# Decay attention, then a feed-forward block: the decay of all jobs from POOL, and the weights converted by block from the second job on

## The chip, the cores and the metric

The kernel runs on one core of one Trainium2 chip. The metric is device time in microseconds (us), the median of the runs. A core has five engines that run side by side, each working through its own list of instructions in order: PE (TensorE, matmuls), DVE (VectorE), ACT (ScalarE), POOL (GpSimd) and SP (which here issues DMAs). POOL and ACT issue DMAs too. All DMAs of the core share 16 DMA engines.

## The reference

Causal attention with a forget gate on 8 batches of 8 heads (576 positions, head size 64), then a feed-forward block on the 4608 resulting rows of 512:

```python
scores = (q @ k.T) / sqrt(64)
cum = cumsum(log(clip(f, 1e-4, 1)))
scores = where(causal, -1e9, scores + cum[i] - cum[j])
attn = exp(scores - max); attn = attn / (sum + 1e-9)
x = attn @ v                                   # (4608, 512)
h = x @ w_in                                   # w_in 512 x 2048
g = h if h >= 1, 0 if h <= -1, else (h + 1)**2 / 4
out = g @ w_out                                # w_out 2048 x 512
```

`w_in` and `w_out` come as 64-bit floats (8 MB each); everything else is 32-bit.

## The kernel before, in words

**Jobs.** The attention is cut into jobs of one pair of heads each (`jobs`; job `p`). Batch 0 has eight jobs: 0 to 3 take rows 0 to 255 of its four head pairs, 4 to 7 take rows 256 to 575. From job 8 on a job is a whole head pair, four jobs to a batch, 36 in all. A job works in blocks of 128 rows (`r`; the last has 64). For a row block, `scores` (L486) makes the products on PE in PSUM, `weights` (L589) takes the row minimum on DVE (L604), the exponential on ACT (L608), normalises, and splits the result into two f16 parts `pr` (ACT L622, DVE L628, or POOL L626); a transposing DMA on SP (L634, L637) brings them to `pT`, and `values` (L641) multiplies with v. Jobs 0 to 4 do the turning on PE instead (`turn_rows`, `early_values`). The values leave PSUM through ACT and DVE (L583/L584 or L657/L658) into `x`.

**The decay.** `decay_sums` (L149) makes the cumulative sums `cum` of log f for all heads and writes them to dram as `cum_d`. There are two ways in which the decay enters the scores. For jobs 0 to 7 (`NDEC`) the sums of batch 0 are also split into three bf16 parts, written to dram as `dec_d`, and each job loads its six rows through SP (`load_decay`, L407; the DMA is L416) into a buffer of the tag `vm`; two more bf16 matmuls per row block add the decay on PE (L511), and the causal mask comes from the prepared tiles `hide` in the minimum on DVE. From job 8 on `load_decay` fetches one row of `cum_d` per head, spread over all partitions, into `ck` (three buffers, POOL's queue, L411); in `scores` POOL makes scale times `ck` plus the row's own sum (L521) and masks the diagonal block (L525), and DVE takes the minimum over that plus the PSUM.

**Scales.** The f16 parts need powers of two as scales. `value_scale(b)` (L274) and `query_scale(b)` (L299) read all of v, q or k of a batch once more in four loads of 288 KB each (POOL's queue; L282, L306) into `vm` buffers, of which there are two, reduce each on DVE (L283, L307), and take the maximum over partitions with `across` (L117: a transpose and a small matmul on PE with small DVE instructions between).

**Weights.** The feed-forward width is cut into 8 blocks of 256. A block of each matrix is 1 MB of 64-bit floats; `weight_load` (L213) fetches it raw on SP into slots (`RAW`), which are partly places where other blocks will lie later; `weight_split` (L225) turns it into 32-bit with three DVE bit operations per quarter (L232, L235, L238), finds a bound (largest magnitude on DVE, L248, for `w_in`; sum of magnitudes on ACT, L252, for `w_out`), takes it through `across`, makes a scale, and writes a high f16 part (ACT L259) and the rest (POOL L261 and L262 for `w_in`, DVE L264 for `w_out`). One call handles one matrix of one block: 16 calls. `CONVERT` says in which job how many are made (jobs 3 to 7), `LOADS` and `AHEAD` how far ahead raw data is fetched.

**Feed-forward.** A unit is 256 rows (`ch`) by one block (`fb`): `moe_front` (L675: 24 or more matmuls into `ph`, then Relu, Square, a DVE clamp L701, and the two f16 parts of g, L703, L704) and `moe_back` (L711: 12 matmuls into `po`). There are 144 units. After each row block of a job so many units are run that those whose rows are ready get used up over four jobs; chunk 0 runs in three groups of blocks (`EARLY`), so that it can begin before all weights are there.

**Order.** The program is written in this order, job by job, with the loads of job p+2 and the preparation of job p+1 in job p. The compiler's scheduler then fixes each engine's list ahead of time: an instruction may be placed long before its turn in the program, once its inputs and a buffer are to be had by the scheduler's own reckoning, and buffers of one tag are handed out in the program's order. At run time each list is worked through in order.

Of the kernel before, what the change touches and what calls it, by code (L numbers as in the profile page):

```python
# [9 lines left out]
F16 = mybir.dt.float16  # L10
BF16 = mybir.dt.bfloat16
I32 = mybir.dt.int32
# [4 lines left out]
P = 128  # L17
# [14 lines left out]
NQK = 12  # L32
NDEC = 8

# [15 lines left out]
def kernel(  # L50
# [9 lines left out]
):  # L60

# [80 lines left out]
    nc.gpsimd.memset(ones, 1.0)  # L142
    NR = 6
    NDH = NDEC // (2 * NPAIR) * H
    dec_d = dram.tile([NDH, NR, 2, S], BF16, name="dec_d")
    cum_d = dram.tile([B * H, S], F32, name="cum_d")
    cq8 = const.tile([P, NT5, B * H], F32, name="cq8")

    def decay_sums():  # L149

        fl = early
        nb = B * H
        nc.sync.dma_start(fl[0:nb, 0:S], f.rearrange("b h s -> (b h) s"))
        rows = one.tile([P, NT5, 2, 2, S], F16, name="pT").rearrange("p t l h s -> p (t l h s)").bitcast(BF16)
        rows = rows[0:NDH, 0:NR * 2 * S].rearrange("p (r j s) -> p r j s", r=NR, j=2)
        nc.gpsimd.memset(fl[0:nb, 3 * S:4 * S], 0.0)
        nc.gpsimd.memset(rows[:, 1::2, 0], 1.0)
        nc.gpsimd.memset(rows[:, 0::2, 1], 1.0)
# [3 lines left out]
        nc.scalar.activation(fl[0:nb, S:2 * S], fl[0:nb, 0:S], AF.Ln)  # L162
        cum = fl[0:nb, 2 * S:3 * S]
# [11 lines left out]
        nc.sync.dma_start(dec_d, rows)  # L175
        nc.sync.dma_start(cum_d, cum)
        pt = ps1.tile([P, 1024], F32, name="big")
        twice = fl[0:nb, S:S + P]
# [12 lines left out]
    hides = one.tile([P, 2, 2, SP], F16, name="qs").rearrange("p j l e -> p (j l e)").bitcast(F32)  # L191
    hide, hide4 = hides[:, 0:FULL], hides[:, FULL:FULL + S]
    for t, h in ((hide, 1), (hide4, 2)):
        n = P // h
        wide = t.shape[1]
        nc.gpsimd.memset(t, 0.0)
        for i in range(h):
            a = t[n * i:n * i + n, wide - n:wide]
            nc.gpsimd.affine_select(
                a, a, pattern=[[-1, n]], channel_multiplier=1, base=0, compare_op=ALU.is_ge, fill=MASKED  # L200
            )

# [7 lines left out]

    def weight_load(n):  # L213
        i, j = divmod(n, 2)
        if j == 0:
            src = w_in.bitcast(I32)[:, i * 4 * P:(i + 1) * 4 * P].rearrange("(t p) c -> p t c", p=P)
        else:
            src = w_out.bitcast(I32)[i * 2 * P:(i + 1) * 2 * P, :].rearrange("(t p) c -> p t c", p=P)
        n = src.shape[1] // 2
        for k_, slot in enumerate(RAW[2 * i + j]):  # L220
            nc.sync.dma_start(
                slots[slot].rearrange("p (t c) -> p t c", t=n), src[:, n * k_:n * (k_ + 1), :]
            )

    def weight_split(n):  # L225
        i, j = divmod(n, 2)
        parts = []
        for k_, slot in enumerate(RAW[n]):
            top = slots[slot][:, 1::2]
# [10 lines left out]
            )  # L240
            parts.append((top.bitcast(F32), slice(k_ * DM, (k_ + 1) * DM)))
        hi = place[n][:, 0]
        lo = place[n][:, 1]
        m1 = tiny.tile([P, 1], F32, name="m1", bufs=2)
        ms = tiny.tile([P, 2], F32, name="ms", bufs=2)
        for k_, (wf, c) in enumerate(parts):
            if j == 0:
                nc.vector.tensor_reduce(  # L248
                    out=ms[:, k_:k_ + 1], in_=wf, axis=AX.X, op=ALU.max, apply_absolute_value=True
                )  # L250
            else:
                nc.scalar.activation(lo[:, c], wf, AF.Abs, accum_out=ms[:, k_:k_ + 1])  # L252
        nc.vector.tensor_reduce(out=m1, in_=ms, axis=AX.X, op=ALU.max)
        m = mi[:, i:i + 1] if j == 0 else tiny.tile([P, 1], F32, name="m2")
        across(m, m1)
        s = sw[:, j, i:i + 1]
        scale_of(s, mp[:, j, i:i + 1], m)
        for wf, c in parts:
            nc.scalar.activation(hi[:, c], wf, AF.Copy, scale=s)  # L259
            if n % 2 == 0:  # L260
                nc.gpsimd.tensor_scalar(out=wf, in0=wf, scalar1=s, scalar2=0.0, op0=ALU.mult, op1=ALU.add)  # L261
                nc.gpsimd.tensor_tensor(out=lo[:, c], in0=wf, in1=hi[:, c], op=ALU.subtract)  # L262
            else:
                nc.vector.scalar_tensor_tensor(  # L264
                    out=lo[:, c], in0=wf, scalar=s, in1=hi[:, c], op0=ALU.mult, op1=ALU.subtract
                )

# [139 lines left out]
    def load_decay(w, h):  # L407
        bh = w.b * H + 2 * w.hp + h
        if w.p >= NDEC:
            ck = two.tile([P, S], F32, name="ck", bufs=3)  # L410
            nc.gpsimd.dma_start(ck, cum_d[bh:bh + 1].broadcast_to([P, S]))  # L411
# [4 lines left out]
        nc.sync.dma_start(w.dec[64 * h:64 * h + NR], dec_d[bh])  # L416

# [68 lines left out]
    def scores(w, r):  # L486
# [15 lines left out]
        w.sds[r] = sds  # L502
        terms = [(x[:, s0:s1], y, D) for x, y in w.qk]
        if w.p < NDEC:
            terms.append((w.dec[:, 0, s0 + w.s0:s1 + w.s0], w.dec[:, 1], NR))
        for c0 in range(0, wid, 512):
            c1 = min(wid, c0 + 512)
            for i, (x, y, n) in enumerate(terms):
                for h in range(2):
                    rows = slice(64 * h, 64 * h + n)  # L510
                    nc.tensor.matmul(  # L511
                        outs[h][:, c0:c1], lhsT=x[rows], rhs=y[rows, c0:c1],
                        start=(i == 0), stop=(i == len(terms) - 1),
                    )
        if w.p < NDEC:
            return
        q0 = P * r
# [71 lines left out]
    def weights(w, r):  # L589
# [172 lines left out]
    def load_weights(n):  # L762
        nonlocal nload
        while nload < min(n, 2 * NB) and not any(set(RAW[nload]) & set(r) for r in RAW[nw:nload]):
            weight_load(nload)
            nload += 1

    def weight_step():
# [5 lines left out]
        for first, end in groups:  # L774
            if nw == 2 * end:
                z = moe_scales(0, first, end - 1, True)
# [13 lines left out]
    for p in range(njobs + 1):  # L790
# [42 lines left out]
        for i, st in enumerate(steps):  # L833
# [3 lines left out]
            while ready() and done - before < quota * (i + 1) // len(steps):  # L837
                if units[done] not in bsc and nw < 2 * NB:
                    break
                moe_unit(*units[done])  # L840
                done += 1
# [35 lines left out]
```

## Time and profile before

| | |
|---|---|
| median of 3 runs | 1243.08 us (1237.45 to 1243.55) |
| the profiled execution | 1248.13 us, span 1246.4 us, mean granted PE clock 0.93 |
| busy share of the span | PE 86%, DVE 67%, ACT 61%, POOL 35% |
| DMA | 163.27 MB, mean 131 GB/s |

The page of the profile gives busy times for each engine and, in 40 slices of 31 us, the busy share in tenths, the granted PE clock and the share of the DMA engines. Other views group instructions by line ("busy, mean ns of one, idle time before them and what ended it"), list them in order of time with their start and length, or give each engine's busy time between two points. In a name like `sdr<-ck,cq` the tile written stands first and those read behind it; PEld is PE's weight load; a suffix q (SPq, POOLq) marks an engine's issuing of DMAs.

### The profile page before, as it was taken

To read this page: it belongs to the slowest core of one execution; us is meant where nothing else is said; L and a number is where in the kernel's file an instruction comes from. 1 tells how busy PE (TensorE), PEld (TensorE's weight loads), DVE (VectorE), ACT (ScalarE), POOL (GpSimd) and SP (SyncE) were. 2 spreads that over 40 slices of the span, in tenths; PEclk is the share of its full clock that TensorE was granted. 3 is DMA by queue.
4 is the path that set the end of the run, shared out by engine and by line. 5 is a ranking of instruction groups with operands and counts; after the bars stand their busy time and mean duration, and the time that the engine had idled before them with its cause. 6 is when DMAs were issued, how large, how long until landed. Compare 5 with 4: busy or idle time off the path is not lost. (4 is left out here: it accounts for less than half of the span.)

```text
span 1246.4 us, 24524 instructions
## 1 busy us (share of the span) xinstructions
PE 1071.5 (86%) x8859; PEld 675.2 (54%) x8859; DVE 830.1 (67%) x2227; ACT 765.8 (61%) x1564; POOL 438.7 (35%) x752
## 2 busy tenths in 40 slices
PE   1569646798327988999999999999999999999998
PEld 1336333454215654665666666656566566667665
DVE  5747879788658777877765576687766877622222
ACT  2456545466436586777766676686777777734443
POOL 2021244464455463544532323454534444100000
PEclk9868767699667998999999999999999999999999
DMA  8822564598999888886756656577777675500000
GB/s 235 277 51 63 143 151 147 143 205 205 180 206 210 179 171 155 163 162 137 147 104 110 127 111 114 120 141 151 141 135 141 128 130 90 93 17 3 18 18 17
DMA packets 404906, 163.27 MB, mean 131 GB/s; under 512 B 384840, under 2 KB 384840, under 8 KB 404776
## 3 DMA queue, kind: packets, MB, share of 16 engines
q1 hardware_dynamic: 389040, 113.33, 48.6%
q0 software_dynamic: 10560, 38.94, 11.6%
q10 hardware_dynamic: 5184, 9.44, 2.1%
q8 instruction: 69, 1.13, 0.4%
q14 instruction: 53, 0.43, 0.1%
HBM read 86.61 MB, written 9.70 MB: 77 GB/s over the span
## 5 line engine op out<-in xcount | busy, mean ns | idle before, releaser
L690 PE MATMUL ph<-x,place 128*128 128x256 f16 (+3 forms) x4608 | 436.1, 249 | 36.9 <-DVE u L701 23.9
L718 PE MATMUL po<-place,g 128*128 128x512 f16 x1728 | 415.9, 383 | 7.1 <-ACT g L703 4.8
L690 PEld LDWEIGHTS <-place 128*128 128x128 f16 x4608 | 355.2, 99 | 115.7 <-issue 41.1
L718 PEld LDWEIGHTS <-g 128*128 128x128 f16 x1728 | 162.3, 99 | 181.3 <-issue 9.5
L521 POOL TENSOR_SCALAR sdr<-ck,nsig,cqs 128x128 f32<-128x128 f32 (+1 forms) x192 | 156.7, 820 | 290.4 <-DVE pr L628 278.0
L608 ACT ACTIVATE sdr<-sdr,nm 128x384 f32<-128x384 f32 (+1 forms) x248 | 137.8, 557 | 117.4 <-DVE nm L604 116.7
L701 DVE SCALAR_TENSOR_TENSOR u<-ph,z,u 128x512 f32<-128x512 f32 x136 | 101.5, 747 | 106.2 <-ACT u L700 105.8
L699 ACT ACTIVATE u<-ph,z 128x512 f32<-128x512 f32 x136 | 104.5, 768 | 76.3 <-PE ph L690 75.4
L628 DVE SCALAR_TENSOR_TENSOR pr<-sdr,rc,pr 128x384 f16<-128x384 f32 (+2 forms) x232 | 122.0, 561 | 38.9 <-ACT pr L622 36.2
L703 ACT ACTIVATE g<-u,z 128x512 f16<-128x512 f32 x136 | 97.7, 719 | 74.0 <-DVE u L701 73.5
L622 ACT ACTIVATE pr<-sdr,rc 128x384 f16<-128x384 f32 (+1 forms) x236 | 119.8, 556 | 34.2 <-ACT sdr L608 14.1
L704 DVE SCALAR_TENSOR_TENSOR g<-u,z,g 128x512 f16<-128x512 f32 x136 | 104.2, 766 | 47.6 <-ACT g L703 47.4
L648 PE MATMUL big<-pT,vs 128*64 128x64 f16 (+3 forms) x1098 | 94.7, 300 | 34.7 <-DMA pT<-pr 33.2
L604 DVE CUSTOM_DVE_ANT_0 sdr<-s,sdr,nalpha 128x128 f32<-128x128 f32 (+1 forms) x192 | 98.5, 546 | 21.3 <-PE s L511 13.1
L511 PE MATMUL s<-qkT 64*128 64x128 f16 (+5 forms) x704 | 91.7, 356 | 20.2 <-DVE nm L604 16.0
L648 PEld LDWEIGHTS <-vs 128*64 128x64 f16 x1098 | 61.5, 117 | 74.5 <-issue 45.6
L700 ACT ACTIVATE u<-u 128x512 f32<-128x512 f32 x144 | 89.7, 624 | 2.4
L525 POOL TENSOR_SCALAR_AFFINE_SELECT sdr<-sdr 128x128 f32<-128x128 f32 x224 | 77.4, 352 | 7.7
L521 POOL TENSOR_SCALAR sd<-ck,nsig,cqs 64x576 f32<-64x576 f32 x48 | 46.1, 960 | 78.2 <-DMA ck<-cum_d 65.5
L511 PEld LDWEIGHTS <-qkT 64*128 64x128 f16 (+1 forms) x864 | 33.2, 99 | 58.2 <-issue 44.6
L433 DVE SCALAR_TENSOR_TENSOR qs<-qk,sqk,qs 128x640 f16<-128x640 f32 x48 | 42.3, 907 | 27.3 <-ACT qs L432 26.9
L432 ACT ACTIVATE qs<-qk,sqk 128x640 f16<-128x640 f32 x48 | 37.1, 819 | 36.2 <-DMA qkT<-qs 30.3
(174 smaller groups left out, 1077.8 us busy)
## 6 DMA issues: line engine op xcount, KB each, us to landing
ck<-cum_d POOLq DMA_DIRECT2D x56, 288.0 KB, 4.7
out_dram<-ot ACTq DMA_DIRECT2D x36, 256.0 KB
qk<-in_k_dram SPq DMA_DIRECT2D x64, 128.0 KB
vm<-in_v_dram POOLq DMA_DIRECT2D x28, 288.0 KB, 3.9
v<-in_v_dram SPq DMA_DIRECT2D x62, 128.0 KB
qk<-in_q_dram SPq DMA_DIRECT2D x56, 128.0 KB
vm<-in_q_dram POOLq DMA_DIRECT2D x24, 288.0 KB, 3.5
vm<-in_k_dram POOLq DMA_DIRECT2D x24, 288.0 KB, 3.8
```

Of the source, the lines that this page charges most:

```text
L511: nc.tensor.matmul(outs[h][:, c0:c1], lhsT=x[rows], rhs=y[rows, c0:c1], start=(i == 0), stop=(i == len(terms) - 1),)
L521: nc.gpsimd.tensor_scalar(out=sd[p0:p1, 0:wid], in0=w.ck[h][p0:p1, 0:wid], scalar1=w.nsig if w.p < NQK else w.nsig[p0:p1], scalar2=w.cqs[p ...
L604: nc.vector.tensor_tensor_reduce(out=a, in0=sp, in1=other, scale=w.nalpha, scalar=BIG, op0=ALU.add, op1=ALU.min, accum_out=nm[:, i:i + 1],)
L608: nc.scalar.activation(a, a, AF.Exp, bias=nm[:, i:i + 1], scale=-1.0, accum_out=sm[:, i:i + 1])
L622: nc.scalar.activation(pr[:, :, 0, i, :], a, AF.Copy, scale=rc[:, i:i + 1])
L628: nc.vector.scalar_tensor_tensor(out=pr[:, :, 1, i, :], in0=a, scalar=rc[:, i:i + 1], in1=pr[:, :, 0, i, :], op0=ALU.mult, op1=ALU.subtract,)
L648: nc.tensor.matmul(av[64 * h:64 * h + 64, at + s0:at + s1], lhsT=w.vs[:, vl, h, t, :], rhs=w.pT[:, t, pl, h, s0:s1], start=(t == 0 and pi ...
L690: nc.tensor.matmul(ph[:, fi, a0:a1], lhsT=wi[fb][:, wl, t, fi * P:(fi + 1) * P], rhs=xs[b][:, t, xl, s0:s0 + a1 - a0], start=(fi == 0 and ...
L699: nc.scalar.activation(u, h, AF.Relu, scale=z.u[:, i:i + 1], bias=z.h[:, i:i + 1])
L701: nc.vector.scalar_tensor_tensor(out=u, in0=h, scalar=z.t[:, i:i + 1], in1=u, op0=ALU.max, op1=ALU.min)
L704: nc.vector.scalar_tensor_tensor(out=g[:, 1], in0=u, scalar=z.r[:, i:i + 1], in1=g[:, 0], op0=ALU.mult, op1=ALU.subtract)
L718: nc.tensor.matmul(po[ch][i], lhsT=g[:, gl, fi * TC + i * P:fi * TC + (i + 1) * P], rhs=wo[fb][:, wl, fi, :], start=(first and fi == 0 and ...
```

## The change

The bf16 path of the decay goes: jobs 0 to 7 get theirs from `ck` and POOL as the others do. For jobs 0 to 11 `ck` is loaded on SP's queue and only as far as the job's rows need it. `weight_split` takes both matrices of a block in one call (8 calls), with one `across` for two columns, and takes all four bounds as sums of magnitudes on ACT; the conversions are made in jobs 1 to 6 instead of 3 to 7, with another table of slots.

```diff
-CONVERT = {3: 3, 4: 3, 5: 4, 6: 4, 7: 2}
-LOADS = {0: 2, 1: 3, 2: 4}
-AHEAD = 4
+CONVERT = {1: 1, 2: 1, 3: 1, 4: 2, 5: 2, 6: 1}
+LOADS = {0: 2, 1: 3}
+AHEAD = 3
 RAW = (
-    (1, 2), (3, 4), (5, 6), (7, 8), (9, 10), (11, 12), (16, 17), (18, 19),
-    (20, 13), (14, 15), (11, 12), (16, 17), (18, 19), (20, 14), (15, 16), (17, 18),
+    (10, 11, 12, 13), (14, 15, 16, 17), (18, 19, 20, 9), (7, 8, 10, 11),
+    (12, 13, 14, 15), (16, 17, 18, 19), (20, 13, 14, 15), (16, 17, 18, 19),
 )
...
 def decay_sums():
...
-        rest = fl[0:NDH, 0:S]
-        nc.vector.tensor_scalar(out=rest, in0=cum[0:NDH], scalar1=8.0, scalar2=None, op0=ALU.mult)
-        for i in range(3):
-            part = rows[:, 2 * i, 0]
-            nc.scalar.activation(part, rest, AF.Copy)
-            nc.scalar.activation(rows[:, 2 * i + 1, 1], part, AF.Copy, scale=-1.0)
-            if i < 2:
-                nc.vector.tensor_tensor(out=rest, in0=rest, in1=part, op=ALU.subtract)
-        nc.sync.dma_start(dec_d, rows)
         nc.sync.dma_start(cum_d, cum)
...
-    def weight_split(n):
+    def weight_split(i):
+        ms = tiny.tile([P, 2, 2], F32, name="ms", bufs=2)
...
+            m = ms[:, k_ // 2, k_ % 2:k_ % 2 + 1]
-            if j == 0:
-                nc.vector.tensor_reduce(
-                    out=ms[:, k_:k_ + 1], in_=wf, axis=AX.X, op=ALU.max, apply_absolute_value=True
-                )
+            if k_ < 0:
+                nc.vector.tensor_reduce(out=m, in_=wf, axis=AX.X, op=ALU.max, apply_absolute_value=True)
             else:
-                nc.scalar.activation(lo[:, c], wf, AF.Abs, accum_out=ms[:, k_:k_ + 1])
+                nc.scalar.activation(low.bitcast(F32), wf, AF.Abs, accum_out=m)
+        m1 = tiny.tile([P, 2], F32, name="m1w", bufs=2)
         nc.vector.tensor_reduce(out=m1, in_=ms, axis=AX.X, op=ALU.max)
+        m = tiny.tile([P, 2], F32, name="m2", bufs=2)
         across(m, m1)
+        nc.vector.tensor_copy(mi[:, i:i + 1], m[:, 0:1])
+        scale_of(sw[:, :, i], mp[:, :, i], m)
...
     def load_decay(w, h):
         bh = w.b * H + 2 * w.hp + h
-        if w.p >= NDEC:
-            ck = two.tile([P, S], F32, name="ck", bufs=3)
-            nc.gpsimd.dma_start(ck, cum_d[bh:bh + 1].broadcast_to([P, S]))
-            w.ck.append(ck)
-            return
-        if h == 0:
-            w.dec = two.tile([P, S], F32, name="vm").bitcast(BF16).rearrange("p (j s) -> p j s", j=2)
-        nc.sync.dma_start(w.dec[64 * h:64 * h + NR], dec_d[bh])
+        ck = two.tile([P, S], F32, name="ck", bufs=3)
+        (nc.sync if w.p < NQK else nc.gpsimd).dma_start(ck[:, 0:w.s1], cum_d[bh:bh + 1, 0:w.s1].broadcast_to([P, w.s1]))
+        w.ck.append(ck)
...
 def scores(w, r):
...
-        if w.p < NDEC:
-            terms.append((w.dec[:, 0, s0 + w.s0:s1 + w.s0], w.dec[:, 1], NR))
...
-        if w.p < NDEC:
-            return
         q0 = P * r
         for h in range(2):
...
 def weights(w, r):
...
-            other = a if w.p >= NDEC else hide[:, FULL - wid:FULL] if r < LAST else hide4
             nc.vector.tensor_tensor_reduce(
-                out=a, in0=sp, in1=other, scale=w.nalpha, scalar=BIG, op0=ALU.add, op1=ALU.min,
+                out=a, in0=sp, in1=a, scale=w.nalpha, scalar=BIG, op0=ALU.add, op1=ALU.min,
```

The high and low f16 parts of the weights are written as before (ACT, then POOL for `w_in` and DVE for `w_out`). The tiles `hide`, their masks and `dec_d` are gone.

More of the change, by code (lines that the diff above doesn't have):

```diff
@@ L142 @@
     nc.gpsimd.memset(ones, 1.0)
-    NR = 6
-    NDH = NDEC // (2 * NPAIR) * H
-    dec_d = dram.tile([NDH, NR, 2, S], BF16, name="dec_d")
     cum_d = dram.tile([B * H, S], F32, name="cum_d")
@@ L153, in decay_sums @@
         nc.sync.dma_start(fl[0:nb, 0:S], f.rearrange("b h s -> (b h) s"))
[L154 to L158, printed above, removed]
         nc.vector.tensor_scalar(
@@ L188, in decay_sums @@
         )
[L191 to L200, printed above, removed]
-            )
     place = [const.tile([P, 2, 2 * DM], F16, name=f"place{i}") for i in range(2 * NB + 1)]
@@ L211, with weight_load @@
     sw = const.tile([P, 2, NB], F32, name="sw")
-    def weight_load(n):
-        i, j = divmod(n, 2)
-        if j == 0:
[L216 to L220, printed above, removed]
+    def weight_load(i):
+        srcs = (
+            w_in.bitcast(I32)[:, i * 4 * P:(i + 1) * 4 * P].rearrange("(t p) c -> p t c", p=P),
+            w_out.bitcast(I32)[i * 2 * P:(i + 1) * 2 * P, :].rearrange("(t p) c -> p t c", p=P),
+        )
+        for k_, slot in enumerate(RAW[i]):
+            src = srcs[k_ // 2]
+            n = src.shape[1] // 2
             nc.sync.dma_start(
-                slots[slot].rearrange("p (t c) -> p t c", t=n), src[:, n * k_:n * (k_ + 1), :]
+                slots[slot].rearrange("p (t c) -> p t c", t=n), src[:, n * (k_ % 2):n * (k_ % 2 + 1), :]
             )
-    def weight_split(n):
-        i, j = divmod(n, 2)
-        parts = []
-        for k_, slot in enumerate(RAW[n]):
+    def weight_split(i):
+        ms = tiny.tile([P, 2, 2], F32, name="ms", bufs=2)
+        wfs = []
+        for k_, slot in enumerate(RAW[i]):
             top = slots[slot][:, 1::2]
@@ L240, in weight_split @@
             )
[L241 to L248, printed above, removed]
-                    out=ms[:, k_:k_ + 1], in_=wf, axis=AX.X, op=ALU.max, apply_absolute_value=True
-                )
-            else:
-                nc.scalar.activation(lo[:, c], wf, AF.Abs, accum_out=ms[:, k_:k_ + 1])
+            wf = top.bitcast(F32)
@@ L255, in weight_split @@
         across(m, m1)
[L256 to L260, printed above, removed]
+        nc.vector.tensor_copy(mi[:, i:i + 1], m[:, 0:1])
+        scale_of(sw[:, :, i], mp[:, :, i], m)
+        for k_, wf in enumerate(wfs):
+            j = k_ // 2
+            s = sw[:, j, i:i + 1]
+            c = slice(k_ % 2 * DM, (k_ % 2 + 1) * DM)
+            hi, lo = place[2 * i + j][:, 0, c], place[2 * i + j][:, 1, c]
+            nc.scalar.activation(hi, wf, AF.Copy, scale=s)
+            if k_ < 2:
@@ L502, in scores @@
         w.sds[r] = sds
-        terms = [(x[:, s0:s1], y, D) for x, y in w.qk]
-        if w.p < NDEC:
-            terms.append((w.dec[:, 0, s0 + w.s0:s1 + w.s0], w.dec[:, 1], NR))
+        terms = [(x[:, s0:s1], y) for x, y in w.qk]
         for c0 in range(0, wid, 512):
             c1 = min(wid, c0 + 512)
-            for i, (x, y, n) in enumerate(terms):
+            for i, (x, y) in enumerate(terms):
                 for h in range(2):
-                    rows = slice(64 * h, 64 * h + n)
+                    rows = slice(64 * h, 64 * h + D)
                     nc.tensor.matmul(
@@ L763, in load_weights @@
         nonlocal nload
-        while nload < min(n, 2 * NB) and not any(set(RAW[nload]) & set(r) for r in RAW[nw:nload]):
+        while nload < min(n, NB) and not any(set(RAW[nload]) & set(r) for r in RAW[nw:nload]):
             weight_load(nload)
@@ L774, in weight_step @@
         for first, end in groups:
-            if nw == 2 * end:
+            if nw == end:
                 z = moe_scales(0, first, end - 1, True)
@@ L837 @@
             while ready() and done - before < quota * (i + 1) // len(steps):
-                if units[done] not in bsc and nw < 2 * NB:
+                if units[done] not in bsc and nw < NB:
                     break
```

13 lines of the change are left out of this document (5 added, 8 removed).

## The prediction

> **What bounds the kernel now.** I read the page first (busy shares, the slices), then a table by stage, then the single rows at the edges of the stages.
>
> ```profile
> PE 1071.5 (86%) x8859; PEld 675.2 (54%) x8859; DVE 830.1 (67%) x2227; ACT 765.8 (61%) x1564; POOL 438.7 (35%) x752
> ...
> DMA  8822564598999888886756656577777675500000
> ```
> ```profile
> core 0: us, PE busy (x) PEld busy (x) DVE busy (x) ACT busy (x) POOL busy (x), PEclk, DMA share, GB/s
> 0.00:36.00 36.00, 6.53 (x24) 3.40 (x24) 22.00 (x45) 8.41 (x13) 9.31 (x25) 1.00 0.81 242
> 36.00:79.00 43.00, 31.84 (x160) 20.48 (x159) 24.32 (x86) 22.36 (x70) 2.00 (x3) 0.80 0.67 198
> 79.00:239.00 160.00, 107.86 (x593) 62.33 (x594) 124.10 (x376) 85.75 (x174) 53.44 (x69) 0.71 0.47 121
> 239.00:280.00 41.00, 37.38 (x256) 21.80 (x255) 35.98 (x113) 26.92 (x61) 22.59 (x40) 0.99 0.79 182
> 280.00:415.00 135.00, 81.28 (x647) 49.76 (x646) 94.62 (x258) 67.67 (x152) 69.37 (x129) 0.79 0.95 194
> 470.00:1096.00 626.00, 610.88 (x5515) 386.03 (x5514) 442.94 (x1183) 448.89 (x918) 252.64 (x439) 0.99 0.69 129
> ```
>
> The stages are cut where a job's values leave PSUM: job 3 at 79 us, job 7 at 239, job 8 at 280, job 12 at 415.
>
> ```profile
> 78.90 0.47 ACT L583 ACTIVATE x<-po,sv 128x256 f16<-128x256 f32 x1 [0.97 <-PE po L576]
> ...
> 238.44 0.44 ACT L657 ACTIVATE x<-big 128x320 f16<-128x320 f32 x1 [8.90 <-PE big L648]
> ...
> 414.98 0.65 ACT L657 ACTIVATE x<-big 128x576 f16<-128x576 f32 x1 [3.70 <-PE big L648]
> ```
>
> From 470 us on PE is busy 611 of 626 us at clock 0.99: nothing there can be had except by PE work, and the change touches none of it. What comes before is not PE-bound. Up to 36 us almost nothing runs on PE; from 79 to 239 us DVE is busy 124 of 160 and PE waits on a lowered clock (0.71); from 280 to 415 us the DMA engines are 0.95 busy and PE only 81 of 135 us. A microsecond saved before 415 us moves the PE-bound rest forward whole.
>
> **The change, part by part.** *1. The first scores.* Now the first job's decay comes as six bf16 rows through a dram copy:
>
> ```profile
> 12.10 1.80 POOL L411 DMA_DIRECT2D ck<-cum_d  x3 [3.95 <-DMA cum_d<-x]
> ...
> 17.51 0.39 SPq L175 DMA_DIRECT2D dec_d<-pT  x1
> ...
> 31.23 1.50 SPq L416 DMA_DIRECT2D vm<-dec_d  x4
> ...
> 35.59 0.47 PE L511 MATMUL s<-vm 6*128 6x128 bf16 x2 [14.52 <-DMA vm<-dec_d]
> ```
> ```profile
> ck<-cum_d POOLq DMA_DIRECT2D x3, 288.0 KB, 7.4
> ```
>
> PE stands 14.5 us for it. After the change the job needs `ck`, whose source is in dram at 12.1 us, 19 us before the row that is waited for now. With the 7.4 us that a `ck` load of that stage took it lands at 19.5; two `tensor_scalar` and two selects (0.67 and 0.35 us, part 3) make 21.5. Gain 14 us; ends: 0, if SP places the load late, and 19 at most. The rows that built the bf16 parts (six on ACT, three on DVE, memsets on POOL, the two `hide` masks) go as well, all inside this wait: nothing. DVE's minimum (L604) reads the POOL tile instead of a mask, one operand for another: nothing.
>
> *2. The ring of `vm` buffers.* Before, `load_decay` takes one of the two `vm` buffers for each of jobs 0 to 7, and `value_scale` and `query_scale` take theirs behind them. These scale loads (76 of 288 KB for batches 1 to 7, no input but q, k, v) are taken long ahead of their jobs as soon as a buffer is free:
>
> ```profile
> 158.57 0.39 PE L511 MATMUL s<-vm 6*128 6x512 bf16 x2
> ...
> 162.65 0.59 POOL L282 DMA_DIRECT2D vm<-in_v_dram  x1 [2.16 <-issue]
> ...
> 207.94 0.39 PE L511 MATMUL s<-vm 6*128 6x512 bf16 x2
> ...
> 208.80 1.07 POOL L306 DMA_DIRECT2D vm<-in_k_dram  x2 [3.71 <-DVE rc L619]
> ```
> ```profile
> L282 POOL DMA_DIRECT2D vm<-in_v_dram x28: 538/574/592, 162.6 to 479.8; - x28
> L306 POOL DMA_DIRECT2D vm<-in_k_dram x24: 538/538/592, 204.6 to 427.2; - x24
> ```
>
> Job 6's last decay matmul ends at 159 and the first load follows at 162.65; job 7's ends at 208.3 and from 208.80 two run at once. (28 from v, 24 each from q and k.) So the ring, not the use, sets their time, and most fall where the DMA is full:
>
> ```profile
> q0 software_dynamic: 3510, 12.94, 36.3%
> ...
> vm<-in_k_dram POOLq DMA_DIRECT2D x12, 288.0 KB, 4.3
> vm<-in_v_dram POOLq DMA_DIRECT2D x12, 288.0 KB, 3.9
> vm<-in_q_dram POOLq DMA_DIRECT2D x12, 288.0 KB, 4.2
> ck<-cum_d POOLq DMA_DIRECT2D x10, 288.0 KB, 5.1
> ```
>
> That is the window 280 to 415: POOL's queue takes 36.3% of the 16 engines, 49 us; 36 of its 46 loads are `vm`, 38 us. After the change no decay holds a `vm`, so the stream can start near 10 us. At its present pace (72 loads in 162 to 427, 3.7 us each; four come later) some 54 are done by 210, against 19 by 239 now (row in part 4). The last 22 would take another 81 us, until 290; job 8 ends some 30 us earlier than now, near 250, so about 11 are left for the stage behind it: of 36 two thirds go, 25 us of DMA. The window's DMA need falls from 128 to 103 us, PE's is 81. I take 20 us; ends: 0 (the window bound by its chain) and 38.
>
> *3. POOL's new work.* Batch 1 (jobs 8 to 11) has the same row blocks as batch 0:
>
> ```profile
> L521 POOL TENSOR_SCALAR sdr<-ck,cq 128x128 f32<-128x128 f32 (+3 forms) x32 | 21.3, 666 | 9.5 <-DVE pr L628 7.3
> L521 POOL TENSOR_SCALAR sd<-ck,cq 64x576 f32<-64x576 f32 x8 | 7.2, 904 | 6.3 <-DMA ck<-cum_d 5.8
> L525 POOL TENSOR_SCALAR_AFFINE_SELECT sdr<-sdr 128x128 f32<-128x128 f32 x56 | 19.3, 349 | 2.2
> L306 POOL DMA_DIRECT2D vm<-in_k_dram x24 | 13.3, 555 | 33.9 <-DVE m L307 16.9 <-DVE gm L107 4.1 <-DVE rc L619 3.7
> ```
>
> 21.3 + 7.2 + 40 x 0.349 = 42 us, in a stretch (36 to 239) where POOL is busy 55 of 203. Costed at nothing while POOL is ahead of DVE; without that cover, rival D. PE loses the 48 bf16 matmuls (0.2 us each by the two above, 9 us, beside idle PE). The 16 new `ck` loads of up to 288 KB at 1.07 us of all engines (49/46) are 13 us of DMA at most, where the share is 0.47: hidden. On SP 24 `ck` issues replace 16 of `dec`; behind each one that waits for a `ck` buffer stand the q, k, v loads and from job 5 the transposes; POOL loses eight issues of jobs 8 to 11. Nothing either way.
>
> *4. The weights.* All conversions go two jobs earlier, as blocks.
>
> ```profile
> L248 DVE TENSOR_REDUCE ms<-place 128x1 f32<-128x512 f32 x12 | 8.0, 677 | 0.1
> L127 DVE TENSOR_REDUCE top<-s 1x1 f32<-1x128 f32 x18 | 4.9, 275 | 5.3 <-PE s L125 5.2
> L252 ACT ACTIVATE place<-place 128x512 f16<-128x512 f32 x10 | 6.6, 661 | 4.5 <-POOL place L262 3.1 <-DVE place L238 1.2 <-DVE place L264 0.2
> L690 PE MATMUL ph<-x,place 128*128 128x256 f16 x205 | 32.6, 312 | 25.7 <-DVE u L701 15.0 <-POOL place L262 4.6 <-DVE m L253 4.0
> ```
>
> DVE loses 16 reductions (16 x 0.677 = 11 us) and eight of 16 cross-partition maxima, each one reduction of 0.275 and seven tiny instructions that I bound by that same 0.275: 2 to 18 us, taken as 11. DVE is 78% busy in 79 to 239, so 22 us less at the same share would be 28. But the `vm` reductions come into this stretch (some 37 more than the 17 of now, 0.74 us each as 56.46 us for 76 below), 27 us that only fill gaps when their data is there. And PE's 8.6 us of waits for `place` and for bounds go, since each MoE group has its blocks a job earlier. I take 15 us; ends: 0 and 36 (DVE never idle). ACT gains 16 sums of 0.66 us, 11 us, in a stage where it is busy 86 of 160: hidden.
>
> ```profile
> 162.00:239.00 77.00, 1.34 (x8) 0.40 (x8) 12.74 (x17) 10.63 (x19) 0.66 0.59 145
> 239.00:415.00 176.00, 0.00 (x0) 0.00 (x0) 36.31 (x49) 27.56 (x49) 0.83 0.91 192
> ...
> sum 1246.00, PE 8.90 PEld 2.60 DVE 56.46 POOL 42.71; mean PE 1.78 PEld 0.52 DVE 11.29 POOL 8.54
> ```
>
> (The view of the `vm` tiles by stage: columns PE, PEld, DVE, POOL; up to 239 us 19 loads and 17 reductions, in 239 to 415 49 of each.)
>
> *5. The price.* The stream's first loads meet a start that is 0.81 busy. Seven of them by 36 us are 7.5 us of DMA (1.07 each) against 7 free, and bursts are uneven: I take 5 us lost; ends 0 and 14 (part 1 gone).
>
> Sum against the profiled execution, 1248.1 us (span 1246.4): 14 + 20 + 15 - 5 = 44, so 1204. That execution stands 5 us above the median of the runs, 1243.1: against the median 1199, forecast **1200**.
>
> **Two rules of the Trainium skill.** The decay's POOL instructions run beside DVE's bit operations. The Trainium skill, SBUF — State Buffer, section Who interferes with whom, says that a DVE instruction with two SBUF inputs contends with a GpSimd one that reads SBUF. Here one such DVE row spreads:
>
> ```profile
> L238 DVE SCALAR_TENSOR_TENSOR place<-place,u x22: 660/692/1897, 17.8 to 194.5; 128x512 int32<-128x512 int32 x22
> ```
>
> The trace allows the rule (1.9 us against 0.69), without naming the cause. By it all 42 us of part 3 could land on DVE and the sum would be 1241 (rival F); by the row's median most pass untouched, and the sum stays.
>
> The Trainium skill, DMA: Bandwidth & Descriptors, section Queues, rings and completion order, says that each DMA engine goes round-robin between queue rows by packet. By that rule the stream gets its turn beside SP's weights whatever is queued there; that is rival C.
>
> **The rivals.** *B, everything is kept:* 19 + 38 + 19 = 76 less 5, so 1172. For it: PE's need in 280 to 415 is only 81 us. Against: rows there also wait for transposes.
>
> *C, the start chokes:* the stream takes its turns from q, k and weights while those are the bottleneck. For it: 0.81 and the 7.4 us landing. It costs the whole gain of part 1 (14) and half of part 4, leaving 20 - 8 = 12: 1231.
>
> *D, slower: POOL's queue holds the decay.* `scores` of jobs 0 to 7 would stand behind scale loads whose buffer waits for a DVE reduction whose data is late. For it: POOL sat 33.9 us before 24 such issues (1.4 us each). Against: POOL is otherwise idle. There are 20 row blocks in four full pairs; held for one turn of the stream (3.7 us) each gives 74 us; it decides from 12 blocks on (44/3.7). With 17 held it is 63 - 44 = 19 slower: 1262.
>
> *E, the stream does not move* (another wait keeps it behind job 7): parts 1 and 4 remain, 29 us: 1214. For it: only that the order on each engine is fixed ahead and may put other work first.
>
> *F, DVE pays for POOL:* two-input rows like L238, which went from 0.69 up to 1.90 us, stretch whenever a decay runs; at 42 us nothing but 2 us is left: 1241. Against: 80 such rows in the conversions, 0.69 each, meet 42 us of POOL in 200, one in five.
>
> **How the numbers follow.** Forecast 0.42, B 0.12, C 0.17, D 0.17, E 0.07, F 0.05. Of C about a third (0.06) lies within 0.5% (6.2 us, what a measurement can tell from no change), of D 0.01, all of F. Faster 0.42 + 0.12 + 0.11 + 0.07 = 0.72, same 0.12, slower 0.16. The range 1168 to 1258 leaves out B's lower and D's upper part, under 2 in 10. The forecast's own range is 1180 to 1222 (each part at half its way to its ends).
>
> **What would show it.** First scores leave PE at 20 to 24 us; the first `vm` load is issued by 15 us and the last before 330; the DMA slices after 280 us fall to 6 to 8; job 7's values come at 205 to 215, job 12's near 370; the PE-bound stretch keeps its length. Wrong, if POOL's rows show the decay idle behind `vm` loads, or if DVE waits for `vm` transfers in the first 100 us.

## The result, and the profile after

The changed kernel takes 1208.25 us (median of four runs, 1207.15 to 1216.61) against 1242.91 us before: ratio 0.9745, 95% interval 0.9694 to 0.9797. The forecast was 1200. The profiled execution took 1207.9 us, span 1206.1 us, against 1248.1 and 1246.4.

The page of the changed kernel:

```profile
PE 1047.8 (87%) x8787; PEld 665.6 (55%) x8787; DVE 817.6 (68%) x2152; ACT 770.2 (64%) x1590; POOL 480.8 (40%) x817
...
DMA  8895756988989788777657556776866664300000
```

The table by stage, cut at the same jobs as before (values of jobs 3, 7, 8 and 12, then the PE-bound stretch), and the rows at which it is cut:

```profile
core 0: us, PE busy (x) PEld busy (x) DVE busy (x) ACT busy (x) POOL busy (x), PEclk, DMA share, GB/s
0.00:36.00 36.00, 11.76 (x46) 7.50 (x46) 23.59 (x60) 13.85 (x37) 11.91 (x34) 1.00 0.88 266
36.00:85.00 49.00, 27.73 (x130) 18.04 (x131) 41.90 (x127) 32.86 (x90) 37.89 (x54) 0.69 0.93 280
85.00:229.50 144.50, 93.94 (x572) 57.70 (x569) 120.59 (x330) 81.45 (x174) 81.22 (x118) 0.82 0.68 178
229.50:257.50 28.00, 25.46 (x186) 15.27 (x186) 20.73 (x54) 20.00 (x44) 14.78 (x29) 1.00 0.88 196
257.50:366.00 108.50, 77.10 (x650) 46.82 (x649) 81.33 (x240) 68.24 (x153) 55.68 (x99) 0.86 0.88 177
420.00:1055.20 635.20, 618.36 (x5563) 390.73 (x5562) 447.44 (x1189) 452.35 (x926) 255.56 (x443) 0.99 0.67 128
```
```profile
84.61 0.45 ACT L538 ACTIVATE x<-po,sv 128x256 f16<-128x256 f32 x1
...
229.01 0.44 ACT L611 ACTIVATE x<-big 128x320 f16<-128x320 f32 x1 [4.02 <-PE big L602]
...
256.88 0.65 ACT L611 ACTIVATE x<-big 128x576 f16<-128x576 f32 x1 [1.51 <-PE big L602]
...
365.31 0.65 ACT L611 ACTIVATE x<-big 128x576 f16<-128x576 f32 x1 [2.35 <-PE big L602]
```

Job 3 ends 6 us later than before (85 against 79), job 7 nine earlier, job 8 23 earlier (257.5 against 280.6). Jobs 8 to 12 take 108.4 us instead of 135.1. Then ten are given back: job 12 to the last job takes 689 us instead of 680, the stretch from 470 on before being 625.5 us and its like here 635.2. So the 40 us come from two places, 23 up to job 8 and 27 behind it, less 10. Job 7's values, forecast for 205 to 215 us, came at 229.5.

The scale loads moved as forecast at their beginning. Their own list, and the view of the `vm` tiles by stage (columns DVE and POOL), of the changed kernel:

```profile
L246 POOL DMA_DIRECT2D vm<-in_v_dram x28: 546/594/713, 2.6 to 434.0; - x28
```
```profile
0.00:257.50 257.50, 39.93 (x54) 32.59 (x56) 0.84 0.78 212
257.50:366.00 108.50, 10.33 (x14) 7.95 (x14) 0.86 0.88 177
366.00:1206.00 840.00, 5.85 (x8) 3.49 (x6) 0.99 0.58 110
```

54 of the 76 reductions lie before job 8's end and 14 in the stage behind it; before, the same view cut at 280.6 and 415.6 has 31 and 35. DMA need in the stage fell from 0.95 of 135 us to 0.88 of 108.5, from 128 to 95 us.

### The profile page after: what moved, and what is told of

The parts are those of the page before. It is cut to its first block, busy times and chain, and to the rows that moved or that the text cites. A ratio compares the mean times of both kernels' runs of the same rounds, so it can differ in the third digit from the quotient of the medians.

```text
span 1206.1 us, 24515 instructions
## 1 busy us (share of the span) xinstructions
PE 1047.8 (87%) x8787; PEld 665.6 (55%) x8787; DVE 817.6 (68%) x2152; ACT 770.2 (64%) x1590; POOL 480.8 (40%) x817
## 5 line engine op out<-in xcount | busy, mean ns | idle before, releaser
L644 PE MATMUL ph<-x,place 128*128 128x256 f16 (+3 forms) x4608 | 432.4, 249 | 19.5 <-DVE u L655 17.2
L468 PE MATMUL s<-qkT 64*128 64x128 f16 (+5 forms) x704 | 88.8, 347 | 33.7 <-DVE nm L558 28.0
L602 PE MATMUL big<-pT,vs 128*64 128x64 f16 (+3 forms) x1098 | 90.7, 293 | 29.0 <-DMA pT<-pr 27.3
L480 POOL TENSOR_SCALAR_AFFINE_SELECT sdr<-sdr 128x128 f32<-128x128 f32 x248 | 91.1, 375 | 8.9
```

The lines of the kernel that those rows point to most:

```text
L468: nc.tensor.matmul(outs[h][:, c0:c1], lhsT=x[rows], rhs=y[rows, c0:c1], start=(i == 0), stop=(i == len(terms) - 1),)
L602: nc.tensor.matmul(av[64 * h:64 * h + 64, at + s0:at + s1], lhsT=w.vs[:, vl, h, t, :], rhs=w.pT[:, t, pl, h, s0:s1], start=(t == 0 and pi ...
L644: nc.tensor.matmul(ph[:, fi, a0:a1], lhsT=wi[fb][:, wl, t, fi * P:(fi + 1) * P], rhs=xs[b][:, t, xl, s0:s0 + a1 - a0], start=(fi == 0 and ...
```

## The experiments

All are compared by where they end job 8, how long jobs 8 to 12 take, and the time from job 12 to the last job (from the ACT rows of the values; the rest is 151 us in each). The ratio is to the kernel before on the same chip.

| kernel | median us | ratio (95%) | job 8 ends | 8 to 12 | 12 to 35 |
|---|---|---|---|---|---|
| before | 1243 to 1249 | 1 | 280.6 | 135.1 | 679.8 |
| b_ownring | 1228.3 | 0.986 (0.980-0.991) | 282.2 | 99.9 | 690.4 |
| b_decay | 1235.8 | 0.991 (0.986-0.995) | 289.6 | 101.9 | 687.1 |
| b_weights | 1214.5 | 0.974 (0.969-0.979) | 246.8 | 129.1 | 689.0 |
| bw_ring | 1215.6 | 0.976 (0.972-0.979) | 260.7 | 103.6 | 697.5 |
| changed | 1208.3 | 0.975 (0.969-0.980) | 257.5 | 108.4 | 689.2 |
| a_hold | 1207.5 | 0.970 (0.965-0.975) | 240.0 | 117.8 | 695.8 |
| a_hold4 | 1209.3 | 0.969 (0.963-0.975) | 247.8 | 112.7 | 698.9 |
| a_null | 1211.7 | 0.974 (0.970-0.978) | 252.4 | 105.8 | 698.8 |
| a_late | 1198.7 | 0.962 (0.959-0.966) | 248.4 | 105.9 | 688.9 |
| a_ringheld | 1182.9 | 0.949 (0.945-0.954) | 238.6 | 99.3 | 691.5 |
| a_convlate | 1203.4 | 0.966 (0.963-0.969) | 251.0 | 106.7 | 692.9 |
| a_dvebound | 1210.4 | 0.972 (0.968-0.976) | 256.2 | 112.9 | 685.9 |
| a_vm3 | 1194.7 | 0.958 (0.954-0.962) | 246.8 | 105.2 | 690.0 |

**The parts alone.** `b_ownring` is the kernel before with the bf16 decay in buffers of its own:

```diff
-            w.dec = two.tile([P, S], F32, name="vm").bitcast(BF16)...
+            w.dec = two.tile([P, S], F32, name="ck", bufs=3).bitcast(BF16)...
```

> The kernel before, with one edit: the bf16 decay rows of jobs 0 to 7 take buffers of the tag ck (three, idle until job 8) instead of vm. Ring theory (the gain comes from the vm buffers that the decay no longer holds): the first scale load is issued before 15 us instead of 162.6, the DMA share in the jobs 9 to 12 falls, and the time drops by 25 to 35 us, to some 1213. Weights theory (it comes from conversions made earlier with less DVE work) and start theory (first scores at 23 us instead of 36): within 6 us of 1243, since neither is touched.

`b_weights` is the kernel before with the weights' part of the diff (`CONVERT`, `LOADS`, `AHEAD`, `RAW`, `weight_load`, `weight_split` and their callers), the decay as before; `b_decay` is the rest of the diff with the weights as before.

> The kernel before with the weights' part of the change alone (blocks, bounds on ACT, conversions in jobs 1 to 6); the decay stays on PE and in vm. Ring theory: gains what less DVE work is worth, 5 to 15 us, to some 1233, with the first scale load still at about 160 us. Weights theory: gains 25 to 35, to some 1212.

> The kernel before with the decay's part of the change alone (POOL and ck for jobs 0 to 7, ck on SP's queue); the weights as before. Ring theory: 20 to 30 us gained, to some 1217. Weights theory: at most 10, to some 1236.

The tables by stage of the own ring, then of the weights alone (up to job 8, and from 8 to 12):

```profile
0.00:282.20 282.20, 182.58 (x1054) 107.48 (x1055) 224.24 (x652) 145.36 (x319) 103.61 (x165) 0.84 0.69 181
282.20:382.10 99.90, 69.40 (x572) 41.62 (x570) 77.23 (x228) 64.33 (x146) 54.37 (x102) 0.81 0.93 195
```
```profile
0.00:246.80 246.80, 167.57 (x1018) 101.60 (x1018) 190.25 (x542) 154.09 (x350) 90.94 (x135) 0.88 0.67 171
246.80:375.90 129.10, 77.46 (x656) 48.41 (x657) 95.65 (x259) 67.05 (x150) 65.99 (x122) 0.80 0.99 207
```

And the same first line of the kernel before:

```profile
0.00:280.60 280.60, 184.20 (x1033) 108.13 (x1033) 207.00 (x621) 144.04 (x317) 87.88 (x137) 0.81 0.59 157
```

The free ring works behind job 8 (135 to 100 us) and not ahead of it, the weights nearly all ahead of it (281 to 247; 6 us behind). DVE says how: the ring puts 23 more reductions ahead of job 8, so DVE is busy 224 us instead of 207, and its idle time falls from 74 to 58: the old gaps take them for nothing. The weights take 17 us of work and 17 us of gaps away (190 busy, 57 idle). The decay part is 7 us slower than its ring alone: 1235.8 against 1228.3, job 8 at 289.6 against 282.2. The theory that the freed ring is the main gain falls: the weights alone give 0.974, as much as the whole change. The ring's own 1228 lies between the two values that were expected for it.

**Both gains at once.** `bw_ring` is `b_weights` with the edit of `b_ownring`.

> The kernel before with the weights' part and a ring of its own for the decay tiles (tag ck, three buffers) instead of vm; the decay stays on PE in bf16. Stage theory with additive parts: job 8 ends at 246 as with the weights alone, jobs 8 to 12 take about 100 us as with the own ring alone, the rest 690, the tail 152: 1190 (1182 to 1200), better than the changed kernel. If the early stream costs the start whenever the weights are converted there too: job 8 at 255 to 265, time 1200 to 1212. If the parts replace each other (what bounds is one common thing): 1210 to 1218, as the weights alone.

`a_hold` is the changed kernel with the old hold on the ring; nothing else differs:

```diff
         w.ck.append(ck)
+        if w.p < 8 and h == 0:
+            w.hold = two.tile([P, S], F32, name="vm")
+            nc.gpsimd.memset(w.hold[:, 0:1], 1e-9)
...
-            nc.vector.tensor_scalar(out=rc[:, 0:nh], in0=sm[:, 0:nh], scalar1=1e-9, scalar2=None, op0=ALU.add)
+            nc.vector.tensor_scalar(out=rc[:, 0:nh], in0=sm[:, 0:nh], scalar1=w.hold[:, 0:1], scalar2=None, op0=ALU.add)
...
-            out=rc[:, 0:nh], in0=sm[:, 0:nh], scalar1=1e-9, scalar2=1.0 / PSC, op0=ALU.add, op1=ALU.mult
+            out=rc[:, 0:nh], in0=sm[:, 0:nh], scalar1=w.hold[:, 0:1] if w.p < 8 else 1e-9, scalar2=1.0 / PSC, op0=ALU.add, op1=ALU.mult
```

> The changed kernel, but each of jobs 0 to 7 holds a vm buffer from its turn until its last row block's sums, as the old decay did: a tiny POOL memset writes the constant 1e-9 into it, and the rc instruction on DVE reads the constant from there. Nothing else is added (16 tiny instructions on POOL and DVE). The scale loads of batches 1 to 7 must then start behind job 6 again. Stage theory (the ring is worth 30 us between the ends of jobs 8 and 12, and the early stream costs some 10 to 20 us before job 8): job 8 ends at 237 to 248 instead of 257, jobs 8 to 12 take 125 to 135 us instead of 108, the time is 1205 to 1222. Rival, ring theory of the prediction alone (free ring only helps): job 8 at 257, time 1228 or more. Rival, order theory (what matters is which order the scheduler happens to find): any time from 1180 to 1225, without the stages moving in opposite directions.

Stages of `bw_ring`, of `a_hold` and, up to job 8, of the changed kernel:

```profile
0.00:260.70 260.70, 166.19 (x969) 100.77 (x970) 207.24 (x576) 151.95 (x347) 101.11 (x165) 0.84 0.75 195
260.70:364.30 103.60, 73.55 (x564) 44.38 (x563) 78.34 (x228) 65.24 (x148) 55.69 (x101) 0.80 0.96 189
```
```profile
0.00:240.00 240.00, 170.88 (x976) 105.35 (x976) 189.90 (x538) 150.04 (x344) 135.77 (x208) 0.87 0.73 188
240.00:357.80 117.80, 71.47 (x539) 41.73 (x539) 90.73 (x251) 63.71 (x145) 62.02 (x120) 0.78 1.03 223
```
```profile
0.00:257.50 257.50, 158.89 (x931) 98.50 (x932) 206.81 (x568) 148.16 (x341) 145.80 (x233) 0.84 0.78 212
```

In both pairs DVE's busy time up to job 8 grows by 17 us (190 to 207), its idle time stays near 50 (57 to 53; 50 to 51), and job 8 ends 14 and 17.5 us later. Behind job 8 the ring gives 25 and 9 us. So in these pairs it is worth about nothing: `a_hold`, without it, takes 1207.5 us. The 1190 of the additive reckoning fell; `bw_ring` ended job 8 where the second theory put it and the whole where the third did.

That the early stream must cost this once the weights are new is not shown. `a_ringheld`, a version with another order, described below, has the stream from 9 us on and as much DVE work, and ends job 8 at 238.6:

```profile
0.00:238.60 238.60, 156.82 (x937) 97.69 (x937) 208.52 (x569) 148.24 (x341) 159.30 (x257) 0.88 0.82 223
```

Nor is it a wait for the stream's transfers: up to job 8 DVE stands 17.2 us for `vm` loads in the changed kernel and 17.3 in `a_hold`, whose first load is issued at 154 us. `a_hold` was to take 125 to 135 us between jobs 8 and 12 and took 118, so the price of a late stream was overrated.

**Holding it for half the time.** `a_hold4` is `a_hold` with 4 for 8.

> The changed kernel with a vm buffer held by each of jobs 0 to 3 only (as in the version with jobs 0 to 7), so that the stream of scale loads starts near 70 us instead of 3 or 154. Stage theory: the start is as with the full hold until job 3, so job 8 ends at 240 to 250; 40 to 45 of the 76 reductions are done by then, so jobs 8 to 12 take 105 to 112 us; time 1190 to 1202, better than both ends. Order theory: anywhere in 1183 to 1215.

Job 8 comes when expected, the stage behind it takes 112.7, and the PE-bound rest then takes 698.9 instead of 689: a miss in the total, and no gain.

**How much is order alone.** `a_ringheld` was the first try at the hold: a memset into the `vm` buffer, and after each row block's scores a copy of it to a spare tile, both on POOL.

```diff
+        if w.p < 8 and h == 0:
+            w.hold = two.tile([P, S], F32, name="vm")
+            nc.gpsimd.memset(w.hold[:, 0:1], 0.0)
...
+        if w.p < 8:
+            nc.gpsimd.tensor_copy(out=freed, in_=w.hold[:, 0:1])
```

> The changed kernel, with each of jobs 0 to 7 again holding one vm buffer until its last scores (an 8th of a microsecond of POOL for each, nothing else). Ring theory: the first scale load comes at about 160 us, and 20 to 30 us of the 35 gained are lost, to some 1235. Weights or start theory: stays within 6 us of 1208.

The copies depend on nothing late, so the scheduler put them all at the start, and the ring was free again after 9 us. POOL's order in time, `a_ringheld` first, then the changed kernel:

```profile
2.63 0.12 POOL L375 MEMSET vm<- 128x1 f32 x2
...
9.39 0.72 POOL L246 DMA_DIRECT2D vm<-in_v_dram  x1
```
```profile
2.64 1.27 POOL L246 DMA_DIRECT2D vm<-in_v_dram  x2
```

So it says nothing of a held ring, yet it is 25 us faster than the changed kernel, outside both expectations. Two more versions ask why. `a_null` has the same memsets and copies on tiles of their own; `a_late` has two instructions more, which keep the first loads until the sums of log f exist:

```diff
         nc.sync.dma_start(cum_d, cum)
+        for _ in range(2):
+            late = two.tile([P, S], F32, name="vm")
+            nc.gpsimd.tensor_copy(out=late[0:nb, 0:1], in_=cum[:, 0:1])
```

> The changed kernel with the same 8 memsets and 20 copies on POOL as in the version with held buffers, but on a tile of their own, so that no vm buffer is touched; POOL's queue issues the first scale loads only some microseconds later, behind the copies. Early-stream theory: between the two, 1185 to 1208, the nearer to 1183 the later the first loads start. Order theory: a null change, and still the time differs from 1208 by more than 6 us in either direction. If added instructions on POOL do not matter and the first loads start at 2.6 to 4 us: 1204 to 1212.

> The changed kernel, but two tiny POOL copies of one column of the cumulative sums into the two vm buffers stand ahead of the first scale loads, so that these can't start before about 9 us (2.6 us in the changed kernel). Two instructions are added. Early-stream theory (the loads at 2.6 us make f, q and k land later and put reductions ahead of the first scores on DVE): f lands near 6 us, the first job's values at 34 to 35 us, job 8 ends at 236 to 245, time 1180 to 1192, like the version with the copies. Order theory: anywhere between 1180 and 1215, job 0's values not tied to the end. Ring theory: no difference, 1205 to 1211.

First loads at 2.6 (changed), 4.5, 8.9 and 9.4 us gave 1208, 1212, 1199 and 1183. `a_null` stays within 4 us of the changed kernel. `a_late` brings job 0's values at 32.6 us (39.1 in the changed kernel), as the early-stream idea had it, but job 8 at 248.4, later than that idea allows. That later first loads help is not excluded, but the two at about 9 us differ by 16 us with the same work but for the tiny instructions. Four such programs, whose lists differ in little but order, spread over 2.5% in time and over 19 us in the end of job 8 (238.6 to 257.5). Against that spread two things stand: all eleven versions with the new weights end job 8 at 238.6 to 260.7 and take 1183 to 1216 us, all three without them at 280.6 to 289.6 and 1228 or more; and jobs 8 to 12 take 118 to 135 us in the three versions whose stream waits for job 6 or 7, 99 to 113 in the others. A single pair that moves job 8 by 14 us does not stand. What in `a_ringheld`'s order is better stays open beyond this: its DVE is idle 30 us up to job 8, the changed kernel's 51.

**What in the weights' part.** `a_convlate` puts the conversions back into jobs 3 to 7, `a_dvebound` the bounds of `w_in` back on DVE:

```diff
-CONVERT = {1: 1, 2: 1, 3: 1, 4: 2, 5: 2, 6: 1}
+CONVERT = {3: 2, 4: 1, 5: 2, 6: 2, 7: 1}
```
```diff
-            if k_ < 0:
+            if k_ < 2:
```

> The changed kernel with the conversions back in jobs 3 to 7 (2, 1, 2, 2, 1 blocks), all else as changed: block form, one maximum over partitions for both matrices, sums on ACT. Timing theory (the gain of the weights' part comes from having the blocks earlier): the last conversion ends near 200 us instead of 170, job 8 ends at 270 to 285 instead of 257, the time is 1225 to 1240. Work theory (it comes from the 22 us that DVE no longer has to do): job 8 within 6 us of 257, 1200 to 1216. The four versions of the changed kernel that differ in nothing but the order so far spread over 1183 to 1212, so a difference below 15 us settles nothing.

> The changed kernel with the bounds of w_in as magnitudes on DVE again (16 reductions of 0.68 us, 11 us) instead of sums on ACT; timing and block form as changed. If DVE's load sets the pace up to job 8: job 8 at 264 to 272, 1216 to 1224. If DVE has room there: 1200 to 1214, within what a mere reordering does.

The second's stage up to job 8:

```profile
0.00:256.20 256.20, 164.18 (x884) 100.25 (x885) 217.97 (x583) 136.70 (x306) 137.79 (x227) 0.77 0.81 212
```

Neither loses anything that the spread would let one see. With the last bit operation of the weights at 193.5 us instead of 168.4, job 8 ends 6 us earlier, not 13 or more later. 11 us more DVE work (218 against 207) go into gaps, job 8 at 256: so the changed kernel's DVE still has gaps to fill. What the two runs leave over of the part is the block form, with the slots and the look-ahead that go with it. Its trace in the views by line, DVE up to job 8: the lines of `across` at which DVE stands, before, in `b_weights` and in the changed kernel.

```profile
L127 DVE TENSOR_REDUCE top<-s 1x1 f32<-1x128 f32 (+1 forms) x19 | 5.2, 275 | 5.3 <-PE s L125 5.2
L136 DVE COPY m<-s 128x1 f32<-128x1 f32 x8 | 1.2, 154 | 7.2 <-PE s L135 7.2
L136 DVE COPY mi<-s 128x1 f32<-128x1 f32 x8 | 1.2, 153 | 4.4 <-PE s L135 4.3
```
```profile
L127 DVE TENSOR_REDUCE top<-s 2x1 f32<-2x128 f32 (+1 forms) x11 | 3.0, 274 | 7.7 <-PE s L125 7.7
L136 DVE COPY m<-s 128x2 f32<-128x2 f32 x8 | 1.2, 148 | 1.3 <-PE s L135 1.2
L136 DVE COPY mv<-s 128x1 f32<-128x1 f32 x2 | 0.3, 152 | 2.7 <-PE s L135 2.7
```
```profile
L123 DVE TENSOR_REDUCE top<-s 2x1 f32<-2x128 f32 (+1 forms) x11 | 3.0, 272 | 0.5 <-PE s L121 0.5
L132 DVE COPY m<-s 128x2 f32<-128x2 f32 x8 | 1.2, 148 | 1.5 <-PE s L131 1.5
```

(Last numbers: idle time before the group, and what ended it.) 19 calls became 11: 16 of the weights became 8, three belong to the scales of v and of q with k. With its shorter lines, which are not shown, `across` costs DVE about 14 us of work and 18 of standing before, 9 and 12 in `b_weights`, 9 and 2 in the changed kernel: DVE, in order, stood for PE's answer. So the blocks by themselves save 11 us of DVE, half of it standing. The other 10 us of standing in the changed kernel go with the same eleven calls, so the fewer calls do not explain them; in `bw_ring` (2.0 us) and `a_hold` (3.1) it is as short, and why stays open. The rest of the 34 us of `b_weights` is not divided by any run: the bounds on ACT and the earlier blocks were taken back only in the changed kernel, where DVE had gaps, and a kernel with blocks but two calls of `across` for each was not run.

**A third buffer.** `a_vm3` is the changed kernel with `bufs=3` on the two `vm` tiles.

> The changed kernel with three vm buffers instead of two, so that a scale load can run one further ahead of its reduction. Early-stream theory (up to job 8 DVE stands behind reductions whose transfer is late, 15 us in 10 waits between 56 and 235 us): these waits fall to 5 us or less and job 8 ends at 242 to 250, 1193 to 1203. If the price of the early stream is the DMA share or the order and not these waits: the waits fall, but job 8 stays at 252 to 262.

The waits of DVE for `vm`, 56 to 235 us, in the changed kernel and with three buffers (columns: us, times, longest):

```profile
DVE m L247 <- DMA vm<-in_v_dram: 10.2, 5, 3.5
DVE m L271 <- DMA vm<-in_k_dram: 3.7, 3, 2.1
...
DVE m L271 <- DMA vm<-in_q_dram: 1.1, 2, 0.8
```
```profile
DVE m L271 <- DMA vm<-in_k_dram: 1.3, 4, 0.4
DVE m L247 <- DMA vm<-in_v_dram: 1.1, 1, 1.1
DVE m L271 <- DMA vm<-in_q_dram: 0.3, 1, 0.3
```

15.0 us of waits become 2.7, job 8 ends at 246.8, 11 us earlier, as expected, and the kernel takes 1194.7. The fall of the waits is shown; that the 13.5 us come from them fits, but is not shown beside an order scatter of that size. `a_hold` has the same waits, so they belong to two buffers rather than to the early stream. This version, `a_late` and `a_ringheld` beat both kernels.

## Why the prediction was right, and where its steps were not

*1, the first scores (14 us):* right where it stands, gone later. The first scores on PE in the changed kernel, then the first row minimum on DVE, which now waits for POOL's decay instead, before and in the changed kernel:

```profile
18.38 0.80 PE L468 MATMUL s<-qkT 64*128 64x128 f32 x4 [1.13 <-DVE mv L132]
```
```profile
36.21 0.29 DVE L604 CUSTOM_DVE_ANT_0 sdr<-s,qs 128x128 f32<-128x128 f32 x1 [0.38 <-PE s L511]
```
```profile
23.16 0.29 DVE L558 CUSTOM_DVE_ANT_0 sdr<-s,sdr 128x128 f32<-128x128 f32 x1 [0.57 <-POOL sdr L480]
```

PE has them at 18.4 us, ahead of the 20 to 24 forecast, since the product no longer waits for any decay; the step's gain is in the minimum, 23.2 instead of 36.2 us, and job 0's values come at 39.1 instead of 52.1, 13 us earlier in both. By job 3 the lead is lost (85.1 against 79.4): from 36 to 85 us DVE is busy 41.9 of 49 us, the DMA share is 0.93, and PE's granted clock is 0.69. The decay without its ring is worth -7 us (`a_hold` against `b_weights`; changed against `bw_ring`) or costs 7 (`b_decay` against `b_ownring`), so this term is 0 within the order scatter. The statement that a microsecond saved before 415 us moves the rest forward whole was the wrong premise: 13 us gained at job 0 are gone at job 3.

*2, the ring (20 us):* the mechanism is right: two thirds were to leave the stage, 35 became 14; job 12 was to come near 370 and ended at 366; the stage fell by 27. The DMA slices behind 280 us stay at 7 to 9 instead of 6 to 8, since the stage got shorter with its need, and the last load is at 434 instead of before 330. What is mis-sized is the price elsewhere: in step 4 the reductions (27 us; 17 measured) were to "only fill gaps when their data is there". They did with the old weights (+2 at job 8 in `b_ownring`); in the two pairs with the new ones job 8 came 14 and 17.5 us later, and how much of that is order stays open.

*3, POOL's decay (0):* right. DVE's first pass over the decay of jobs 0 to 11, changed kernel:

```profile
L558 DVE CUSTOM_DVE_ANT_0 sdr<-s,sdr 128x384 f32<-128x384 f32 (+3 forms) x56 | 26.6, 501 | 3.9 <-POOL sdr L480 3.5 <-PE s L468 0.4
```

These 56 of its 72 rows wait 3.5 us for POOL in all, the others 1.1, although POOL itself stands 74 us ahead of scale loads up to 235 us. So rival D (the queue holds the decay) has no place.

*4, the weights (15 us):* the term that was most too small. At job 8 the weights' part gives 34 us alone, 21.5 beside the free ring (`b_ownring` to `bw_ring`) and 32 beside the whole decay part (`b_decay` to the changed kernel). The step reckoned 28 for DVE's lesser work and then took 15, in view of the stream's reductions. It put the maxima at the length of their instructions (2 to 18 us, taken as 11) and gave nothing for DVE standing between them: `b_weights` saves 5 us of instructions and 6 of standing, 11 by luck, and the changed kernel 5 and 16. Its other reasons, the 11 us of reductions and the earlier blocks, are worth nothing measurable in the changed kernel.

*5, the crowded start (-5):* the first two scale loads are issued at 2.64 us, and DVE's first row of f starts at 7.31 us instead of 6.15. Rival C (the early stream takes back the start's gain) is like what the two pairs show at job 8, 14 and 17.5 us, but as reductions on DVE, not as weights that come late, and other orders do not show it. Its 1231 does not follow from its own terms: 44 less 14 and less half of part 4 leaves 22, so 1221.

*A term that was missing:* the give-back. Every version that shortens the first 415 us takes 6 to 19 us more from job 12 on: in the changed kernel's stretch PE is busy 618.4 us with 5563 matmuls instead of 610.4 with 5513, so most of its ten us are feed-forward matmuls that had been done in the old gaps before.

So 44 was forecast from 14, 20, 15 and -5; measured 40 in the trace, which one way of adding up the runs makes about 0, 27 less 17, 34 and -10, with some 6 that no step accounts for and that order alone can make. The direction and the two mechanisms (ring behind job 8, weights ahead of it) were right; that the total came within 8 us is luck, by errors that cancel. Rival B's 1172 needed gains that add (it took 19 for the weights where the step's own end was 36, without a reason); E (the stream stays) fell by the first load at 2.64 us.

*Rival F, DVE beside POOL:* small, not nil. Rows by line of the changed kernel:

```profile
L204 DVE SCALAR_TENSOR_TENSOR x<-x,u 128x512 int32<-128x512 int32 x11 | 11.0, 1005 | 0.0
...
L230 DVE SCALAR_TENSOR_TENSOR place<-x,sw,place 128x512 f16<-128x512 f32 x6 | 7.5, 1258 | 0.3 <-ACT place L225 0.3
```

At 0.68 and 0.75 us a row they would take 7.5 and 4.5, so 6.5 us go here. All 80 such rows of the conversions take 64.6 us, 9 more than at their median lengths (3 more before); not 42.

## What to carry to other kernels

Gains of two changes to one stage need not add: alone the ring and the weights gave 1.4 and 2.6%, together 2.4%. Count what an in-order engine stands for between the instructions of a small chain, not the instructions alone, and look for it in the run that has this part alone. Where a scheduler fixes the order, run a few versions that differ in order only before a part of the change is credited with less than their spread.

## What the runs showed of the hardware

A DVE row with two SBUF inputs can last as long as a whole series of POOL instructions beside it. The longest one of the changed kernel, on DVE and on POOL:

```profile
168.36 4.08 DVE L204 SCALAR_TENSOR_TENSOR x<-x,u 128x512 int32<-128x512 int32 x1
```
```profile
168.33 0.72 POOL L227 TENSOR_SCALAR place<-place,sw 128x512 f32<-128x512 f32 x1
...
169.62 1.16 POOL L228 TENSOR_TENSOR place<-x,place 128x512 f16<-128x512 f32 x1
170.72 1.15 POOL L228 TENSOR_TENSOR place<-place,place 128x512 f16<-128x512 f32 x1
```

It takes 4.08 us instead of 0.68, from POOL's L227 until 0.6 us behind the second L228. The Trainium skill, SBUF — State Buffer, section Who interferes with whom, says that such a pair contends; this trace agrees, without naming the cause, and has its longest rows beside the weights' own POOL steps (L227, L228), not beside the decay that the prediction feared.
